# Four early layer-1 halves, experts in pairs, and longer store runs in an attention and expert kernel

## The chip, the core and the metric

The kernel runs on one core of a Trainium2 chip. The metric is the device time of one execution in microseconds; lower is better. The engines of the core are named as in the profile: PE (TensorE, the matmuls; PEld is its weight load), DVE (VectorE), ACT (ScalarE), POOL (GpSimd) and SP (SyncE). Transfers are issued from SP, ACT and POOL and carried out by 16 DMA engines.

## What is computed

Attention over 4 batches, 8 heads, 768 positions and head dimension 64, followed by an expert layer in which each token goes to the one expert that its domain names. Heads 0, 2 and 6 see all earlier positions; the other five see only the first 4 positions (the sinks) and the last 64.

```python
scores = q @ k.T / sqrt(64)             # per batch and head
mask   = causal & (retrieval_head | (pos_k < 4) | (pos_q - pos_k < 64))
x      = softmax(where(mask, scores, -1e9)) @ v      # -> 3072 tokens x 512
for e in range(8):                      # w1[e]: 512 x 1024, w2[e]: 1024 x 512
    rows = domain_id == e
    out[rows] = relu(x[rows] @ w1[e]) @ w2[e]
```

All inputs and the output are fp32 in DRAM.

## The kernel before

Attention is worked off in 16 passes: pass n is a batch (n // 4) with a pair of heads (n % 4). The pairs are (0, 2), (6, 7), (1, 3) and (4, 5). A pass has 6, 5, 3 and 3 rounds, one for each tile of scores of up to 1024 columns (`scores`, L293): mask matmuls, then matmuls of kT and qT into PSUM, then the exponential on ACT into a tile `eT` from `epool`. Between the rounds of pass n TensorE also works off `t_items(n + 1)` (transposes of the next pair's q and k, which DVE copies out as qT and kT) and `av_items(n - 1)` (the exponentials times v, into an accumulator of `ps_a`, which DVE divides by the row sums into `xb`, L398 and L399). `hooks(n)` stands ahead of each pass: it issues the q, k and v loads of pass n + 4 on SP, the casts to fp16 on POOL (L155, L176), and, in some passes, a store of a finished batch (`store_x`, L411, on SP) or a weight load (`load_w`, L181 for the first layer, L187 for the second, on POOL). A weight is 2 MB of fp32 in DRAM and becomes 1 MB of fp16 on its way. The text writes (3,1) for the first-layer weight of expert 3.

The tokens are sorted meanwhile. `routing_items` yields a list of small steps on DVE, among them 24 comparisons of 128 by 128 (`low`, L575), one group of matmuls (`table`) and, at the end, `rows` and `rows2`, which make `map_i` (the row of x for each slot) and `out_i` (the row of the output for each slot). One step is taken after each round from pass 1 on.

The experts work on slots. Each has 448, 384 main and 64 more; a pair of experts has 7 groups of 128 slots: groups 0 to 2 are the main slots of the first expert, 3 to 5 those of the second, 6 the two remainders. `load_xe` (L631) gathers a group's rows of x by an indirect DMA from POOL; `x_transpose` (L647) turns them into `xT`; `layer1` (L671, L678) makes `hT` with relu on ACT; `layer2` (L702) and `layer2_half` (L716) multiply with the second weight, and `finish_group` copies a group of 128 rows out of PSUM into one of four `oute` tiles (L684, on DVE) and scatters it to the output by an indirect DMA from POOL (L686).

The first 256 slots of an expert come from the first three batches, if it has so many tokens there. `N_EARLY` experts use that: their groups 0, 1, 3 and 4 are gathered in pass 14 (with rows of three batches only), and `layer1(e, 0, EARLY)` covers columns 0 to 255 while the last batch's rows are stored and gathered; `layer1(e, EARLY, CAP)` follows. A flag (`flag_i`) tells of an input for which this, or the 448 slots, isn't enough; a loop at the end then does everything again in a plain way.

Nothing is scheduled by a planner: each engine runs its instructions in the order in which the program issues them. POOL's order therefore sets the order of weights, gathers and scatters:

```python
ws = {4: (0, 1), 8: (1, 1), 11: (0, 2), 12: (2, 1)}        # load_w in hooks(n)
if n == 14:
    for g in (0, 1, 3, 4):
        load_xe(0, g, 3)
    load_w(1, 2)
```

After the passes, layer 1 of expert e + 2 is issued ahead of layer 2 of expert e, for each e in turn, and each weight is loaded as soon as its buffer (four for each layer) is free.

Of the kernel before, what the change touches and what calls it, by code (L numbers as in the profile page):

```python
# [9 lines left out]
FP16 = mybir.dt.float16  # L10
# [11 lines left out]
def kernel(  # L22
# [26 lines left out]
    MAIN = 384  # L49
    HALF = CAP - MAIN  # L50
    EARLY = 256
    N_EARLY = 2
    PAIRSLOTS = 2 * CAP
    NSLOT = E * CAP
    PAIRS = [(0, 2), (6, 7), (1, 3), (4, 5)]
# [56 lines left out]
    vpool = ctx.enter_context(tc.tile_pool(name="v32", bufs=4))  # L112
    vepool = ctx.enter_context(tc.tile_pool(name="ve", bufs=2))
    tpool = ctx.enter_context(tc.tile_pool(name="qkT", bufs=2))
    epool = ctx.enter_context(tc.tile_pool(name="eT", bufs=3))
    xpool = ctx.enter_context(tc.tile_pool(name="xb", bufs=2))
    mpool = ctx.enter_context(tc.tile_pool(name="moe", bufs=3))
    opool = ctx.enter_context(tc.tile_pool(name="moe_out", bufs=4))
# [178 lines left out]
    def scores(n, r):  # L297
        chunks, c0, c1 = plans[n % 4][r]
        sp = ps_s.tile([P, 1024], FP32, tag="sp", name=f"sp_{n}_{r}")
        lists = {0: [], 1: [], 2: []}  # L300
        for ch in chunks:
            lists[ch[1]].append(ch)
        order = []
        for a, c in zip(lists[0] + [None] * 8, lists[1] + [None] * 8):
            order += [x for x in (a, c) if x]
        masks = masks_of(n, r)
        begun = set()

        def put(c, w, lhsT, rhs):
            bank = c // 512  # L310
            nc.tensor.matmul(  # L311
                out=sp[:, c : c + w],
                lhsT=lhsT,
                rhs=rhs,
                start=bank not in begun,
                stop=True,
                skip_group_check=True,
            )
            begun.add(bank)

        for c, w, col in masks:
            put(c, w, id_sb, c16[:, col : col + w])
        for c, hh, jt, i0, w in order + lists[2]:
            if hh == 2:
                put(c, w, ks_t[n % 2][:], qT[n][:, i0 : i0 + w])
            else:
                rows = slice(64 * hh, 64 * hh + 64)
                j0 = 0 if jt == "s" else jt * P
                put(c, w, kT[n][rows, j0 : j0 + P], qT[n][rows, i0 : i0 + w])
        if r == 0:  # L330
            eT[n] = epool.tile([P, 6, 1024], FP16, tag="eT", name=f"eT_{n}")
        nc.scalar.activation(  # L332
            out=eT[n][:, r, c0:c1], in_=sp[:, c0:c1], func=AF.Exp, scale=scale
        )

    def masks_of(n, r):
# [15 lines left out]
    def av_items(n):  # L352
# [3 lines left out]
        for hh, h in enumerate(PAIRS[pi]):  # L356
# [15 lines left out]
            def mm(x, h=h, hh=hh, mms=mms, cell=cell, both_s=both_s):  # L372
                it, jt, m0, m1 = mms[x]
                if x == 0:
                    cell["ps"] = ps_a.tile([P, 512], FP32, tag="av", name=f"av_{n}_{hh}")
                ps = cell["ps"][:, 0 : NSO * (D + 1)].rearrange("p (t d) -> p t d", t=NSO)
                r, c = col_of(tiles, hh, jt, it * P + m0)
                w = m1 - m0
                if jt == "s":
                    if both_s and hh == 1:  # L380
                        kk, rhs = slice(32, 36), vs_t[b][32:36, h, :]
                    else:
                        kk, rhs = slice(0, NS), ve_t[b][0:NS, 0, h, :]
                else:
                    kk, rhs = slice(0, P), ve_t[b][:, jt, h, :]
                nc.tensor.matmul(  # L386
                    out=ps[m0:m1, it, :],
                    lhsT=eT[n][kk, r, c : c + w],
                    rhs=rhs,
                    start=(x == 0),  # L390
                    stop=(x == len(mms) - 1),
                    skip_group_check=True,
                )
                if x == len(mms) - 1:
                    if b not in xb:
                        xb[b] = xpool.tile([P, NSO, DM], FP16, tag="xb", name=f"xb_{b}")
                    rcp = tpool.tile([P, NSO], FP32, tag="rcp", name=f"rcp_{n}_{hh}")
                    nc.vector.reciprocal(out=rcp[:], in_=ps[:, :, D])  # L398
                    nc.vector.tensor_tensor(  # L399
                        out=xb[b][:, :, h * D : (h + 1) * D],  # L400
                        in0=ps[:, :, 0:D],
                        in1=rcp[:].unsqueeze(2).to_broadcast([P, NSO, D]),
                        op=ALU.mult,
                    )
# [4 lines left out]

    def store_x(b):  # L410
        nc.sync.dma_start(  # L411
            out=x_d[1 + b * S : 1 + (b + 1) * S, :].rearrange("(t p) d -> p t d", p=P), in_=xb[b][:]
        )


    def routing_items():
# [32 lines left out]
        ohh = mpool.tile([P, NT, 2, NHI], FP16, tag="xT", bufs=4, name="ohh")  # L449
        mf = tile_([P, 2, NHI], FP32, "mf")  # L450
        me = tile_([P, NHI], FP32, "me")

        def one_hot():
            V.tensor_tensor(
# [143 lines left out]

        def rows2():
            V.tensor_scalar(  # L600
                out=mf[:, 1, :], in0=me[:], scalar1=float(NT - 1), scalar2=float(1 - NT),
                op0=ALU.mult, op1=ALU.add,
            )
            V.tensor_tensor(out=mf[:, 1, :], in0=mf[:, 0, :], in1=mf[:, 1, :], op=ALU.add)
            V.tensor_copy(out=map_i[:], in_=mf[:, 1, :])
            V.scalar_tensor_tensor(
                out=me[:], in0=me[:], scalar=2.0 * NTOK, in1=mf[:, 1, :],
                op0=ALU.mult, op1=ALU.add,
            )
            V.tensor_scalar(  # L610
                out=out_i[:], in0=me[:], scalar1=1.0, scalar2=None, op0=ALU.subtract
            )

        idle = lambda: None
# [2 lines left out]
            add(fn)  # L617
        for t in range(0, NT, 2):
            add(lambda t=t: (low(t), low(t + 1)))
        for fn in (idle, table, rows, rows2):  # L620
            add(fn)
        return items

    xe_t, xT_t, hT_t = {}, {}, {}
    NG = PAIRSLOTS // P

    def load_xe(pr, g, nb=B):
        if pr not in xe_t:
            xe_t[pr] = vepool.tile([P, NG, DM], FP16, tag="ve", name=f"xe_{pr}")
        s = pr * NG + g  # L630
        nc.gpsimd.indirect_dma_start(  # L631
            out=xe_t[pr][:, g, :],
            out_offset=None,
            in_=x_d[0 : 1 + nb * S, :],
            in_offset=bass.IndirectOffsetOnAxis(ap=map_i[:, s : s + 1], axis=0),
            bounds_check=nb * S,
            oob_is_err=False,
        )

    def x_transpose(pr, g):  # L640
# [4 lines left out]
        for c in range(4):  # L645
            c1, r = divmod(c, 2)
            nc.tensor.transpose(  # L647
                out=ps[:, c, :],
                in_=xe_t[pr][:, g, c1 * 256 + r : (c1 + 1) * 256 : 2],
                identity=id_sb,  # L650
            )
        if g < 6:
# [8 lines left out]

    def layer1(e, c0, c1):
        if e not in hT_t:
            hT_t[e] = epool.tile([P, 8, CAP], FP16, tag="eT", name=f"hT_{e}")
        for f2 in range(4):
            ps = ps_s.tile([P, 1024], FP32, tag="sp", name=f"h1_{e}_{f2}_{c0}")
            pv = ps[:].rearrange("p (a c) -> p a c", a=2)
# [83 lines left out]
    def hooks(n):  # L751
# [9 lines left out]
            vs_copy(b)  # L761
        if n >= 5 and n % 4 == 1:
            store_x(n // 4 - 1)
        ws = {4: (0, 1), 8: (1, 1), 11: (0, 2), 12: (2, 1)}
        if n in ws:
            load_w(*ws[n])
        if n == 14:
            for g in (0, 1, 3, 4):
                load_xe(0, g, 3)
            load_w(1, 2)  # L770

    for _, fn in t_items(0):
        fn()
    route = routing_items()
    for n in range(NPAIR + 1):
        if n < NPAIR:
            hooks(n)
# [8 lines left out]
        for r in range(R):  # L786
            if n < NPAIR:
                scores(n, r)
            if n >= 1 and route:
                route.pop(0)()  # L790
            while x < len(bg) and (done < total * (r + 1) / R - 1 or r == R - 1):
                done += bg[x][0]
                bg[x][1]()
                x += 1
        if n == NPAIR - 1:
            for g in (0, 1, 3, 4):
                x_transpose(0, g)

    store_x(B - 1)
    for g in (2, 6, 5):  # L800
        load_xe(0, g)
    for e in range(N_EARLY):
        layer1(e, 0, EARLY)
    load_w(3, 1)
    for g in range(4):
        load_xe(1, g)
    load_w(2, 2)
    for g in range(4, NG):
        load_xe(1, g)
    for g in (2, 6, 5):  # L810
        x_transpose(0, g)
    for e in range(N_EARLY):
        layer1(e, EARLY, CAP)
        load_w(e + 4, 1)
        if e == 0:
            load_w(3, 2)
    for e in range(E):
        pr, i = divmod(e, 2)
        nxt = e + 2
        if i == 1:  # L820
            layer2_half(pr)
        if nxt < E:
            if i == 0:
                for g in range(7):
                    x_transpose(pr + 1, g)
                if pr + 2 < E // 2:
                    [load_xe(pr + 2, g) for g in range(NG)]
            layer1(nxt, 0, CAP)
            if nxt + 4 < E:
                load_w(nxt + 4, 1)  # L830
        layer2(e)
        if e + 4 < E:
            load_w(e + 4, 2)


    with tc.If(nc.values_load(flag_i[0:1, 0:1], min_val=0, max_val=2) > 0, preferred_fallthrough_block=False):  # L836
        with tc.For_i(0, NT, 1) as t:
            g_d64 = rpool.tile([P, 1], I64, name="g_d64")
            nc.sync.dma_start(
                out=g_d64[:], in_=moe_domain_id[bass.ds(t * P, P)].rearrange("(p c) -> p c", c=1)  # L840
# [1 line left out]
            g_dom = rpool.tile([P, 1], FP32, name="g_dom")  # L842
            nc.vector.tensor_copy(out=g_dom[:], in_=g_d64[:].bitcast(I32)[:, 0:1])
            gx = vepool.tile([P, DM], FP16, tag="ve", name="gx")
            nc.sync.dma_start(out=gx[:], in_=x_d[bass.ds(t * P + 1, P), :])
            gps = ps_t.tile([P, NSO, P], FP16, tag="tp", name="gps")
            for c in range(4):
                c1, r = divmod(c, 2)
# [81 lines left out]
```

## Time and profile before

| What | Value |
|---|---|
| median of 5 runs | 241.78 us (240.82 to 242.83) |
| profiled execution | 242.02 us, of which 240.2 us are the span from the first to the last instruction |
| mean granted TensorE clock | 0.935 |
| PE, PEld busy | 203.2 us (85%), 120.5 us (50%) |
| DVE, ACT, POOL busy | 105.6, 92.7, 110.3 us |
| POOL's DMA queue | 26.75 MB, 48.5% of the 16 engines' span |
| SP's DMA queue | 22.02 MB, 33.5% |
| L671 PE, first layer | 320 matmuls, 53.1 us |
| L702 PE, second layer | 192 matmuls, 42.6 us |
| L631 POOL, gathers | 28, 28.4 us of issue |
| L686 POOL, scatters | 28, 27.9 us of issue |

A row of the page names line, engine and operation, what is written and read, then busy time, the mean of one and the idle time of the engine ahead of it with its releaser. In the rows for a stretch of time the columns are its length, then for each engine (PE, PEld, DVE, ACT, POOL) the busy time and the number of instructions, then the granted clock of TensorE as a share, the share of the DMA engines that was busy, and GB/s. Attention ends at 109 us on TensorE, and its last matmul of all ends at 231.5 us.

### The profile page before, as it was taken

Reading aid. Unit: us, or ns where it says so; the run is one execution under the profiler, and the core shown is the slowest. Engines: PE = TensorE matmul, PEld = TensorE weight load, DVE = VectorE, ACT = ScalarE, POOL = GpSimd, SP = SyncE. Lnnn points to the kernel's source line nnn. Section 1 sums busy time; section 2 is a strip of 40 time slices with the busy share of each in tenths; the row PEclk is TensorE's granted clock in tenths of the full one; section 3 lists DMA queues with packets and bytes.
Section 4 is the critical chain, followed back from the end, with each engine's and each line's share of the span. In section 5 each row is a group of like instructions: output and inputs, shape, how many; then the busy total and the mean of one; then the engine's idle time right before and its main releaser. Section 6 shows DMA issues by size and latency. Waiting matters only on the chain. (4 is left out here: it accounts for less than half of the span.)

```text
span 240.2 us, 4605 instructions
## 1 busy us (share of the span) xinstructions
PE 203.2 (85%) x1871; PEld 120.5 (50%) x1871; DVE 105.6 (44%) x242; ACT 92.7 (39%) x109; POOL 110.3 (46%) x143
## 2 busy tenths in 40 slices
PE   1489969996999999989582699997999889999950
PEld 0246545664556666669471354545545455454420
DVE  1349999997546956761202203125040431303330
ACT  2177538762647687635260041320505023140000
POOL 0647565454413760701778612737545321505540
PEclk9999998998559999999998579999999999999996
DMA  6999999999999998285499999999977873303320
GB/s 220 297 317 290 286 287 248 298 334 285 232 301 299 268 191 220 66 165 168 96 252 221 198 213 263 149 263 220 277 226 182 212 158 68 134 3 122 130 107 23
DMA packets 45467, 49.77 MB, mean 207 GB/s; under 512 B 27263, under 2 KB 38784, under 8 KB 45442
## 3 DMA queue, kind: packets, MB, share of 16 engines
q0 software_dynamic: 7936, 26.75, 48.5%
q1 hardware_dynamic: 36928, 22.02, 33.5%
q10 hardware_dynamic: 578, 0.66, 0.9%
q8 instruction: 16, 0.26, 0.4%
q14 instruction: 9, 0.07, 0.1%
HBM read 56.76 MB, written 10.49 MB: 280 GB/s over the span
## 5 line engine op out<-in xcount | busy, mean ns | idle before, releaser
L332 ACT ACTIVATE eT<-sp 128x1024 f16<-128x1024 f32 (+2 forms) x68 | 60.7, 916 | 39.1 <-PE sp L311 38.5
L678 ACT ACTIVATE hT<-h 128x896 f16<-128x896 f32 (+2 forms) x40 | 30.7, 768 | 79.6 <-PE h L671 79.6
L671 PE MATMUL h<-xT,w 128*128 128x448 f16 (+2 forms) x320 | 53.1, 326 | 1.2 <-DVE xT L657 1.2
L686 POOL DMA_INDIRECT out_dram<-oute,out_i x28 | 27.9, 995 | 39.3 <-DVE oute L684 36.4
L684 DVE COPY oute<-o 128x512 f32<-128x512 f32 x24 | 16.6, 692 | 66.5 <-PE o L702 66.5
L631 POOL DMA_INDIRECT xe<-x_tok,map_i x28 | 28.4, 1015 | 33.5 <-SPq L836 10.8
L671 PEld LDWEIGHTS <-w 128*128 128x128 f16 x320 | 34.1, 115 | 19.1 <-issue 4.1
L702 PE MATMUL o<-w,hT 128*128 128x512 f16 x192 | 42.6, 379 | 0.0
L386 PE MATMUL av<-ve,eT 128*128 128x65 f16 (+3 forms) x532 | 32.3, 199 | 2.8 <-DVE xb L399 2.8
L386 PEld LDWEIGHTS <-eT 128*128 128x128 f16 (+3 forms) x572 | 26.2, 102 | 14.0 <-issue 4.6
L311 PE MATMUL sp<-qT,kT 64*128 64x192 f16 (+6 forms) x244 | 27.7, 291 | 3.1 <-DVE fl L542 1.9
L702 PEld LDWEIGHTS <-hT 128*128 128x128 f16 x192 | 18.7, 98 | 22.4 <-issue 0.4
L155 POOL CAST q<-q 128x768 f16<-128x768 f32 x15 | 12.9, 862 | 32.7 <-issue 13.0
L311 PE MATMUL sp<-c16s 128*128 128x128 f16 (+1 forms) x132 | 26.6, 285 | 0.6 <-ACT eT L332 0.5
L647 PE MATMUL xtp<-c16s,xe 128*128 128x128 f16 x112 | 10.5, 228 | 12.4 <-DMA xe<-x_tok,map_i 9.5
L281 DVE COPY qT<-tpq 128x768 f16<-128x768 f16 x16 | 15.3, 955 | 8.3 <-PE tpq L276 8.3
L311 PEld LDWEIGHTS <-kT 64*128 64x128 f16 x244 | 9.9, 96 | 18.0 <-issue 7.5
L155 POOL CAST k<-k 128x768 f16<-128x768 f32 x16 | 13.5, 843 | 11.0 <-DMA k<-in_k_dram 9.4
L399 DVE TENSOR_TENSOR xb<-av,rcp 128x384 f16<-128x384 f32 x32 | 17.8, 557 | 1.1
L654 DVE COPY xT<-xtp 128x512 f16<-128x512 f16 x24 | 9.3, 420 | 19.8 <-PE xtp L647 18.8
L281 DVE COPY kT<-tpk 128x768 f16<-128x768 f16 x16 | 15.2, 949 | 3.5 <-PE tpk L276 3.5
L176 POOL CAST ve<-v 128x384 f16<-128x384 f32 x32 | 15.9, 525 | 0.7 <-DMA v<-in_v_dram 0.7
(71 smaller groups left out, 124.5 us busy)
## 6 DMA issues: line engine op xcount, KB each, us to landing
w<-in_moe_w_dram POOLq DMA_DIRECT2D x16, 1024.0 KB, 10.4
q<-in_q_dram SPq DMA_DIRECT2D x16, 384.0 KB, 6.0
k<-in_k_dram SPq DMA_DIRECT2D x16, 384.0 KB, 6.0
v<-in_v_dram SPq DMA_DIRECT2D x32, 192.0 KB, 5.9
x_tok<-xb SPq DMA_DIRECT2D x4, 768.0 KB, 5.9
xe<-x_tok,map_i POOLq DMA_INDIRECT x28, 7.2
out_dram<-oute,out_i POOLq DMA_INDIRECT x28, 2.8
c16s<-c ACTq DMA_DIRECT2D x1, 336.5 KB, 4.5
```

What stands on the lines that cost most here:

```text
L155: eng.tensor_copy(out=t[:].rearrange("p t h d -> p h t d"), in_=q32_t[nm, n][:])
L281: nc.vector.tensor_copy(out=d[:], in_=cell["ps"][:].rearrange("d t p -> d p t"))
L311: nc.tensor.matmul(out=sp[:, c : c + w], lhsT=lhsT, rhs=rhs, start=bank not in begun, stop=True, skip_group_check=True,)
L332: nc.scalar.activation(out=eT[n][:, r, c0:c1], in_=sp[:, c0:c1], func=AF.Exp, scale=scale)
L386: nc.tensor.matmul(out=ps[m0:m1, it, :], lhsT=eT[n][kk, r, c : c + w], rhs=rhs, start=(x == 0), stop=(x == len(mms) - 1), skip_group_check ...
L399: nc.vector.tensor_tensor(out=xb[b][:, :, h * D : (h + 1) * D], in0=ps[:, :, 0:D], in1=rcp[:].unsqueeze(2).to_broadcast([P, NSO, D]), op=A ...
L631: nc.gpsimd.indirect_dma_start(out=xe_t[pr][:, g, :], out_offset=None, in_=x_d[0 : 1 + nb * S, :], in_offset=bass.IndirectOffsetOnAxis(ap= ...
L671: nc.tensor.matmul(out=pv[:, a, c0:c1], lhsT=w_t[e, 1][:, c // 2, c % 2, fc * 512 + fr : (fc + 1) * 512 : 4], rhs=xT_t[e][:, c, c0:c1], st ...
L678: nc.scalar.activation(out=hT_t[e][:, 2 * f2 : 2 * f2 + 2, c0:c1], in_=pv[:, :, c0:c1], func=AF.Relu)
L684: nc.vector.tensor_copy(out=o[:], in_=ps[:])
L686: inst = nc.gpsimd.indirect_dma_start(out=out, out_offset=bass.IndirectOffsetOnAxis(ap=out_i[:, s : s + 1], axis=0), in_=o[:], in_offset=None,
L702: nc.tensor.matmul(out=ps[:], lhsT=hT_t[e][:, f, g * P : (g + 1) * P], rhs=w_t[e, 2][:, f // 4, f % 4, :], start=(f == 0), stop=(f == 7),)
```

## The change

It has these parts.

- `N_EARLY` becomes 4: experts 0 to 3 do their first 256 columns ahead. The early gathers of pairs 0 and 1 stand in pass 14, each pair's four followed by a weight, (2,1) and (3,1). Weights (0,2), (2,1) and (1,2) leave passes 11, 12 and 14.
- The gathered rows get other buffers (`xe_of`: those of q and k for groups 0 to 5, those of v for group 6). The early ones are cleared by four memsets on DVE in pass 14.
- The transposes of pair 0's early groups move from ahead of the last attention matmuls to behind them.
- Experts go in pairs: both layer 2 of a pair, then the loads, then both layer 1 of the pair after the next. In POOL's queue (4,1), (2,2), (5,1) and (3,2) stand one behind the other, and so do (6,1), (4,2), (7,1) and (5,2).
- x is stored so that each partition's six rows lie together: 6 KB in one run, where it was 1 KB. `rows2` and the new `rows3` compute the row of x for it.
- The routing takes a step in two of three rounds.
- `epool` has five smaller buffers instead of three; `eT` of a pass takes one or two of them.
- POOL gets a drain behind the last two weights.

```diff
-    N_EARLY = 2
+    N_EARLY = 4
-    epool = ctx.enter_context(tc.tile_pool(name="eT", bufs=3))
+    epool = ctx.enter_context(tc.tile_pool(name="eT", bufs=5))
...
-        if r == 0:
-            eT[n] = epool.tile([P, 6, 1024], FP16, tag="eT", name=f"eT_{n}")
+        if r % 3 == 0:
+            t = epool.tile([P, 8 * CAP], FP16, tag="eT", name=f"eT_{n}_{r}")
+            eT[n, r // 3] = t[:, 0 : 3 * 1024].rearrange("p (r c) -> p r c", r=3)
...
     def store_x(b):
         nc.sync.dma_start(
-            out=x_d[1 + b * S : 1 + (b + 1) * S, :].rearrange("(t p) d -> p t d", p=P), in_=xb[b][:]
+            out=x_d[1 + b * S : 1 + (b + 1) * S, :].rearrange("(p t) d -> p t d", p=P), in_=xb[b][:]
         )
...
+    def xe_of(pr, g):
+        u, o = (2 * pr + g // 3, g % 3) if g < 6 else ((pr, "h"), 0)
+        if u not in xe_t:
+            if g < 6:
+                xe_t[u] = qkpool.tile([P, 3, DM], FP16, tag="qk"[u % 2], name=f"xe_{u}")
+            else:
+                xe_t[u] = vpool.tile([P, 1, DM], FP16, tag="v32", name=f"xeh_{pr}")
+        return xe_t[u][:, o, :]
...
-        ws = {4: (0, 1), 8: (1, 1), 11: (0, 2), 12: (2, 1)}
+        ws = {4: (0, 1), 8: (1, 1)}
         if n in ws:
             load_w(*ws[n])
         if n == 14:
-            for g in (0, 1, 3, 4):
-                load_xe(0, g, 3)
-            load_w(1, 2)
+            for pr in range(2):
+                for i in range(2):
+                    xe_of(pr, 3 * i)
+                    nc.vector.memset(xe_t[2 * pr + i][:, 0:2, :], 0.0)
+            for pr in range(2):
+                for g in (0, 1, 3, 4):
+                    load_xe(pr, g, 3)
+                load_w(2 + pr, 1)
...
             if n >= 1 and route:
-                route.pop(0)()
+                rounds += 1
+                if rounds % 3:
+                    route.pop(0)()
...
-        if n == NPAIR - 1:
-            for g in (0, 1, 3, 4):
-                x_transpose(0, g)
-
     store_x(B - 1)
-    for g in (2, 6, 5):
-        load_xe(0, g)
-    for e in range(N_EARLY):
-        layer1(e, 0, EARLY)
-    load_w(3, 1)
...
+    for g in (0, 1, 3, 4):
+        x_transpose(0, g)
+    for g in (2, 5, 6):
+        load_xe(0, g)
+    load_w(0, 2)
+    for g in (2, 5, 6):
+        load_xe(1, g)
+    load_w(1, 2)
+    for g in range(NG):
+        load_xe(2, g)
+    layer1(0, 0, EARLY)
+    for g in (0, 1, 3, 4):
+        x_transpose(1, g)
+    for e in range(1, N_EARLY):
+        layer1(e, 0, EARLY)
...
+    for pr in range(2):
+        for g in (2, 5, 6):
+            x_transpose(pr, g)
+        for e in (2 * pr, 2 * pr + 1):
+            layer1(e, EARLY, CAP)
+            if e < 2:
+                load_w(e + 4, 1)
+                load_w(e + 2, 2)
+    for pr in range(E // 2):
+        a, b_ = 2 * pr, 2 * pr + 1
+        layer2(a)
+        layer2_half(pr)
+        layer2(b_)
+        for e in (a, b_):
+            if e + 6 < E:
+                load_w(e + 6, 1)
+            if e + 4 < E:
+                load_w(e + 4, 2)
+        if pr == 1:
+            nc.gpsimd.drain()
+        if pr + 3 < E // 2:
+            for g in range(NG):
+                load_xe(pr + 3, g)
+        if pr + 2 < E // 2:
+            for g in range(NG):
+                x_transpose(pr + 2, g)
+            layer1(a + 4, 0, CAP)
+            layer1(b_ + 4, 0, CAP)
```

`rows2` and `rows3` have ten small DVE operations together, where `rows2` had five; the loop at the end reads x by the new order.

## The prediction

> **What bounds the kernel now.** I read the page first (busy tenths, clock, DMA), then the stretches by engine and clock, the waits of TensorE, its timeline from 100 us on, and last the issues and landings of the GpSimd queue. The page:
>
> ```profile
> span 240.2 us, 4605 instructions
> PE   1489969996999999989582699997999889999950
> DVE  1349999997546956761202203125040431303330
> PEclk9999998998559999999998579999999999999996
> DMA  6999999999999998285499999999977873303320
> ```
>
> TensorE (203.2 us busy of 240.2) is the bound nearly everywhere, so the question is where it idles and where its clock is low. Two holes show: slices 5, 6 and 9 with the half clock of slices 11 and 12, and slices 19 to 23. The DMA row is near full up to slice 31 and offers no free room before 180 us. The stretches:
>
> ```profile
> 20.00:40.00 20.00, 16.95 (x229) 10.69 (x228) 19.22 (x51) 11.36 (x13) 13.11 (x21) 0.91 1.12 284
> 40.00:60.00 20.00, 17.80 (x267) 11.59 (x265) 18.14 (x54) 11.73 (x14) 8.60 (x14) 0.97 1.11 299
> ...
> 58.80:72.40 13.60, 13.60 (x109) 7.71 (x107) 6.51 (x15) 7.23 (x8) 4.07 (x6) 0.50 1.10 270
> 130.50:140.70 10.20, 7.10 (x27) 3.32 (x28) 1.34 (x4) 0.92 (x1) 6.02 (x6) 0.50 1.05 208
> ```
>
> From 20 to 60 us VectorE (fourth column, 37.4 of 40 us) is full while TensorE idles 5.2 us: the routing shares VectorE with attention. Then TensorE is busy for 13.6 us at half clock. The second half-clock stretch follows the hole in the expert stage:
>
> ```profile
> PE xtp L647 <- DMA xe<-x_tok,map_i: 9.5, 6, 4.5
> ...
> 131.74 1.03 PE L647 MATMUL xtp<-c16s,xe 128*128 128x128 f16 x8 [4.52 <-DMA xe<-x_tok,map_i]
> 134.25 0.61 PE L647 MATMUL xtp<-c16s,xe 128*128 128x128 f16 x4 [1.48 <-DMA xe<-x_tok,map_i]
> 135.24 8.90 PE L671 MATMUL h<-xT,w 128*128 128x448 f16 x32 [0.39 <-DVE xT L657]
> ...
> 151.11 6.24 PE L671 MATMUL h<-xT,w 128*128 128x448 f16 x32
> ```
>
> Between 115 and 136 us TensorE waits 9.5 us for gathered rows, and the first full layer 1 takes 8.90 us instead of 6.24: 2.7 us more for the clock. All gathers, weights and scatters go through one GpSimd queue:
>
> ```profile
> 127.85 0.79 POOL L181 DMA_DIRECT2D w<-in_moe_w_dram  x1
> 128.59 0.81 POOL L187 DMA_DIRECT2D w<-in_moe_w_dram  x1
> 129.32 0.79 POOL L181 DMA_DIRECT2D w<-in_moe_w_dram  x1
> ...
> 126.00:130.00 4.00, 1.07 (x12) 0.71 (x12) 1.57 (x4) 0.00 (x0) 3.69 (x5) 1.00 1.06 214
> ```
>
> With weights alone in flight the core moves 214 GB/s, and a weight is 1.05 MB as stored: 4.9 us each. The third of these weights lands 19.6 us after its issue (148.9), a gather issued behind it at 131.79 lands 17.9 us after its own: the queue delivers in order. A lone weight takes 8.1 us to landing, a lone gather 2.8, a lone scatter 2.7. A scatter issued at 155.24 behind one weight took 11.0.
>
> **The change, part by part.**
>
> 1. Routing in two rounds of three (rounds % 3). Routing costs VectorE some 19 us up to the table matmul: 24 ohl at 0.32 us (7.7) and single operations of 0.13 to 0.93. Before, all of that and the first row step lie in passes 1 to 7; now about 15.3 us do, the rest moves to passes 8 to 11: 4.4 us less for VectorE before 58 us. Passes 10 and 11 are short: 4.1 to 4.5 us of TensorE each against about 4 of VectorE without routing (qT and kT 0.95 each, ks 0.3, two of 0.20 plus 0.56, vs 0.3), and get rows, rows2 and rows3 (13 operations of some 0.18). That gives back about 1.4. Net -3.0. Bounds: 0, if the transfers pace attention (q15 lands at 81.6 and its cast runs at 86.0 now, so only 4.4 us of slack), and -5.5, if the half-clock stretch of 58.8 to 72.4 goes with the idle time before it. At 109 matmuls in 13.6 us against about 14.5 per us at full clock that stretch costs some 6 us, which the slack caps.
>
> 2. Four memsets of xe (hook 14) on VectorE. From the rows of 64 and 256 words (112 and 272 ns), 512 words take about 0.49: 1.95 us in the queue ahead of qT and kT of pass 15. 0.62 us of idle time stands there; kT then ends at about 100.3, its first use is at 100.78. The softmax division at 99.59 ends 1.3 late and holds an accumulator: +0.4. Without that cover, +1.9. The first gather waits for the first memset and starts near 97.2, against 96.74.
>
> 3. Transposes of pair 0 behind the last attention matmuls: 1.82 us of TensorE (104.38 to 106.20) move out of the path to the last store, so attention ends at 106.2 and the store goes out at 107.1; in SP's queue nothing stands behind it. No work is saved.
>
> 4. The 6 KB runs. Now the store of 0.79 MB lands 3.7 us after issue on an idle DMA, 6.0 among other transfers; the stretch that moves it runs at 348 GB/s with 1 KB runs. The Trainium skill (DMA: Bandwidth & Descriptors, Specifications) holds that 512 bytes are already enough for line rate. By the row the longer run can save at most a few tenths of the 2.3 us of transfer, by the rule nothing. I take nothing. Against it: the store now meets weights (2,1) and (3,1) in flight, which it did not before. I take 5 us (between 3.7 and 6.0).
>
> 5. Early halves for four experts. Each costs 3.62 us (7.24 for two now); the halves are 0.2 us dearer than a whole layer 1 per expert, 0.4 for the two new ones. In the time of this trace: attention 106.2, transposes 108.1, half 0 111.7; pair 1's early gathers lie behind weight (2,1), issued at 102.4 and landing at 110.5, the last gather at 112.0: wait 0.4; transposes 114.0; halves 1 to 3 124.9; the last batch's gathers, behind (3,1), have landed by 119; transposes 126.9; two rests of 2.84 132.6; transposes 134.6; rests 140.3. The 9.5 us of waiting are gone.
>
> 6. Weights and scatters. GpSimd issues the gathers of pairs 0, 1 and 2 (1.3 us each) with (0,2) and (1,2) until 132, then (4,1), (2,2), (5,1), (3,2) in a row. They land at about 140, 145, 150 and 155. Layer 2 of expert 0 runs from 140.3 to 145.5 and its scatters are issued at once, but stand behind these four weights: they land from 155. There are four oute buffers; the fifth copy (expert 1, first group) waits for the first scatter. With two accumulators TensorE then stops at the third group of expert 1, at 150.9, for 5.1 us. Now the same fifth copy waits for one weight only and its wait ends as its matmuls do (159.0). Afterwards (6,1), (4,2), (7,1), (5,2) are issued behind the last scatter of pair 0, from 160; they land until 182.5, pair 3's gathers until 185, scatters of pair 1 behind them (the first is also held at its issue until (5,2) has landed, since each issue of this queue waits for the eighth before it): 1.8 us of waiting at 184.6. Pair 3's transposes (188.1) find their rows. The end of TensorE is 229.1 with a store of 6 us, 228.2 with 5, against 231.5.
>
> 7. The clock after that stop. The skill (TensorE: Matmul & The Clock Gate, Part 1) lets the clock fall to half after one idle window of about 3.4 us and return after one busy one: 1.7 us lost. The trace shows less mercy: after the idle 4.5 us the clock stayed at 0.50 for 10.2 us, about 5 lost if all of it is work. A stop of 5.1 us should trip it. A slower TensorE also eats the 1.8 us of waiting that comes later. I take +1.5, between 0 and +5.
>
> 8. The drain after (7,2): GpSimd's next work is a scatter some 20 us later. Nothing; were it on the path, one issue, 1 us. The fallback loop isn't entered: in the drawn input the first four experts have 285 to 311 tokens in three batches, and none has over 448. epool has five buffers, eT takes six per four passes and always finds one free.
>
> **Sum.** Against the profiled run (240.2 us span, 242.02 us with what lies around it): 231.5 to 228.2 is -3.3, attention -3.0, memsets +0.4, clock +1.5: -4.4, so 235.8 span and 237.6. The median of the runs is 241.78, 0.24 under that run: 237.4.
>
> **Rivals.** (a) The half clock in attention goes too and the stop at 151 us stays short (the store lands in 3.7): attention -5.5, expert stage -4.6, memsets +0.4, clock +0.7: -9.0, so 232.8. For it: the idle 2.4 us of 53 to 58 stand directly before the fall. Against: the DMA row is full there.
> (b) Slower: the scatters behind four weights. If a weight takes 5.6 us beside scatters and gathers instead of 4.9 (154 to 157 us ran at 162 GB/s), the eight that stand before expert 0's scatters come 5.6 us later, the stop is 10.7 us, and the clock costs its 5: with attention -1, 241.8 - 3.3 + 5.6 + 5 + 0.4 - 1 = 248; with half of that, 245. It decides from about 9 us of stop and slow clock together.
> (c) No change: the routing only moves its pressure to passes 8 to 11 (0 instead of -3), the rest as computed, with the clock at +3: 241.8.
>
> **How the numbers follow.** The likeliest, 0.40, gives 237.4 (its own range 235 to 239.5); (a) 0.26; (b) 0.21; (c) 0.13. A measurement here tells apart about 0.5%, 1.2 us. Faster: 0.40 + 0.26 and a little of (c): 0.68; same 0.11; slower 0.21. The range from 231.5 to 245 takes in most of (a) and the lower half of (b).
>
> **What would show it.** Right: attention's last matmuls by 104; no wait on gathers between 110 and 136; VectorE's copies of oute for expert 1 waiting for a scatter near 150, with TensorE idle 3 to 5 us and the clock low behind it; (6,1) issued after 157. Wrong: no such wait of oute (the queue is not in order, or the weights landed sooner), or no shorter attention, or transposes of pair 1 still waiting for rows.

## The result and the profile after

The changed kernel takes 241.51 us (median of 42 runs, 237.99 to 248.34), the kernel before 241.60 (79 runs); the ratio is 0.995 [0.993, 0.997]. Ratios leave disturbed runs out, so they need not be the ratio of the medians, and oute7_shifted below, with too few undisturbed runs, has none. Forecast: 237.4, -1.8%. Measured: -0.5%. Two later comparisons of the same two kernels gave 0.991 [0.987, 0.995] and 0.990 [0.984, 0.996].

The page of the changed kernel (its own time 241.94 us, its span 240.1):

```profile
PE   1489989699989999999988994068999479999990
DVE  1347999999969768532022040025003160033431
PEclk9999999999997999959999998559999999999997
DMA  6999999999999431799799899935999649813322
```

The holes at slices 19 to 22 (counted from 0) are gone. In their place stands one at slices 24 to 26, deeper than any before, with the half clock behind it, and a small one near slice 31. The DMA row now has a gap of its own at slices 13 to 15, and is full from there to slice 24. By stretches (length; busy time and instructions of TensorE, weight loads, VectorE, ScalarE, GpSimd; granted clock; DMA share; GB/s):

```profile
20.00:40.00 20.00, 18.67 (x268) 12.09 (x265) 17.82 (x51) 13.62 (x17) 12.24 (x21) 1.00 1.13 288
40.00:60.00 20.00, 17.96 (x257) 11.27 (x254) 19.52 (x47) 13.01 (x15) 11.60 (x18) 1.00 1.12 304
80.00:98.00 18.00, 17.44 (x249) 10.93 (x247) 13.13 (x28) 13.16 (x16) 8.38 (x11) 1.00 0.21 72
98.00:157.00 59.00, 46.65 (x427) 36.98 (x427) 11.30 (x28) 19.17 (x34) 26.52 (x28) 0.87 0.98 210
100.90:107.80 6.90, 6.66 (x50) 5.06 (x48) 2.87 (x8) 0.66 (x2) 2.78 (x3) 0.51 1.04 280
148.70:162.40 13.70, 4.20 (x16) 2.00 (x16) 1.92 (x3) 0.00 (x0) 1.97 (x2) 0.50 0.71 181
```

From 20 to 60 us TensorE idles 3.4 us where it was 5.2. From 80 to 98 us the DMA carries 72 GB/s; from 98 to 157 it is full at 210 GB/s. That is the queue that the stop hangs on. TensorE's timeline:

```profile
110.84 10.74 PE L701 MATMUL h<-xT,w 128*128 128x256 f16 x96
...
135.84 5.34 PE L732 MATMUL o<-w,hT 128*128 128x512 f16 x24
...
142.96 3.63 PE L732 MATMUL o<-w,hT 128*128 128x512 f16 x16
158.20 3.57 PE L732 MATMUL o<-w,hT 128*128 128x512 f16 x8 [11.61 <-DVE oute L714]
...
191.63 1.89 PE L732 MATMUL o<-w,hT 128*128 128x512 f16 x8 [3.24 <-DVE oute L714]
...
228.77 5.36 PE L732 MATMUL o<-w,hT 128*128 128x512 f16 x24
```

The early halves run without a wait for rows. Layer 2 of expert 1 stops for 11.6 us on a copy of oute, and expert 3 for 3.2. The waits say what that copy waited for. The landings of the three scatters of expert 0 from 138 to 144 us say how long those took, the one below them that of the last of the four weights ahead of them in the queue, and the last that of attention's last store:

```profile
DVE oute L714 <- DMA out_dram<-oute,out_i: 19.5, 3, 13.7
PE o L732 <- DVE oute L714: 14.8, 2, 11.6
```

```profile
L716 POOL DMA_INDIRECT out_dram<-oute,out_i x3: 982/1039/1068, 138.7 to 142.2; - x3
...
DMA to landing us min/median/max: 16.4/17.5/18.6
...
L187 POOL DMA_DIRECT2D w<-in_moe_w_dram x1: 750/750/750, 134.2 to 134.2; - x1
...
DMA to landing us min/median/max: 22.4/22.4/22.4
...
L412 SPq DMA_DIRECT2D x_tok<-xb x1: 357/357/357, 102.9 to 102.9; - x1
...
DMA to landing us min/median/max: 7.8/7.8/7.8
```

The span in three parts, before and after: to attention's last matmul 108.11 and 102.07 us (-6.04); from there to the last matmul of all 123.35 and 132.05 (+8.70); from there to the end 8.78 and 5.94 (-2.84). Together -0.2. A second profile of the changed kernel (after_again, 239.23 us) has 99.7, 131.9 and 5.7 us, with a stop of 10.9 us. The third part is the surprise: it lies behind all work, and is GpSimd's last drain (durations min/median/max in ns). Before, and then after, with the added drain first:

```profile
L925 POOLq DRAIN  x3: 46/109/6100, 233.3 to 240.0; - x3
```

```profile
L868 POOLq DRAIN  x1: 16961/16961/16961, 195.3 to 195.3; - x1
...
L970 POOLq DRAIN  x3: 50/103/2932, 236.3 to 239.8; - x3
```

### The profile page after: what moved, and what is told of

Read it like the earlier page. It is cut to its first block, busy times and chain, and to the rows that moved or that the text cites. A ratio compares the mean times of both kernels' runs of the same rounds, so it can differ in the third digit from the quotient of the medians.

```text
span 240.1 us, 4769 instructions
## 1 busy us (share of the span) xinstructions
PE 200.3 (83%) x1935; PEld 125.3 (52%) x1935; DVE 107.5 (45%) x251; ACT 93.6 (39%) x117; POOL 110.1 (46%) x143
## 5 line engine op out<-in xcount | busy, mean ns | idle before, releaser
L708 ACT ACTIVATE hT<-h 128x512 f16<-128x512 f32 (+2 forms) x48 | 32.1, 668 | 78.4 <-PE h L701 78.4
L732 PE MATMUL o<-w,hT 128*128 128x512 f16 x192 | 44.6, 390 | 14.8 <-DVE oute L714 14.8
L701 PE MATMUL h<-xT,w 128*128 128x256 f16 (+2 forms) x384 | 52.2, 297 | 1.6 <-DVE xT L686 1.6
L701 PEld LDWEIGHTS <-w 128*128 128x128 f16 x384 | 39.7, 115 | 13.2 <-DVE xT L686 1.7
L660 POOL DMA_INDIRECT xe<-x_tok,map_i x24 | 24.4, 1018 | 26.0 <-DVE xe L801 7.8
L387 PE MATMUL av<-ve,eT 128*128 128x65 f16 (+3 forms) x532 | 31.4, 197 | 5.0 <-DVE xb L400 3.1
L311 PE MATMUL sp<-qT,kT 64*128 64x192 f16 (+6 forms) x244 | 26.1, 277 | 1.4 <-DVE kT L281 1.4
L311 PE MATMUL sp<-c16s 128*128 128x128 f16 (+1 forms) x132 | 25.9, 277 | 0.4 <-ACT eT L333 0.2
L276 PE MATMUL tpq<-c16s,q 128*128 128x128 f16 x96 | 9.4, 237 | 6.0 <-DVE q L155 5.2
## 6 DMA issues: line engine op xcount, KB each, us to landing
w<-in_moe_w_dram POOLq DMA_DIRECT2D x16, 1024.0 KB, 11.6
```

What stands on the lines that cost most here:

```text
L311: nc.tensor.matmul(out=sp[:, c : c + w], lhsT=lhsT, rhs=rhs, start=bank not in begun, stop=True, skip_group_check=True,)
L387: nc.tensor.matmul(out=ps[m0:m1, it, :], lhsT=eT[n, r // 3][kk, r % 3, c : c + w], rhs=rhs, start=(x == 0), stop=(x == len(mms) - 1), skip ...
L660: nc.gpsimd.indirect_dma_start(out=xe_of(pr, g), out_offset=None, in_=x_d[0 : 1 + nb * S, :], in_offset=bass.IndirectOffsetOnAxis(ap=map_i ...
L701: nc.tensor.matmul(out=pv[:, a, c0:c1], lhsT=w_t[e, 1][:, c // 2, c % 2, fc * 512 + fr : (fc + 1) * 512 : 4], rhs=xT_t[e][:, c, c0:c1], st ...
L708: nc.scalar.activation(out=hT_t[e][:, 2 * f2 : 2 * f2 + 2, c0:c1], in_=pv[:, :, c0:c1], func=AF.Relu)
L732: nc.tensor.matmul(out=ps[:], lhsT=hT_t[e][:, f, g * P : (g + 1) * P], rhs=w_t[e, 2][:, f // 4, f % 4, :], start=(f == 0), stop=(f == 7),)
```

## The experiments

They ran on five chips, A to E, each with the kernel before beside them. "Halves to layer 2" is the time in the profile from the start of the halves of experts 1 to 3 to the start of layer 2; in the changed kernel it is 25.0 (110.84 to 135.84).

| kernel | chip | median us | ratio to before | halves to layer 2 |
|---|---|---|---|---|
| oute7 | A | 237.0 | 0.984 [0.976, 0.992] | 29.4 |
| two_behind | A | 243.3 | 1.004 [0.999, 1.009] | 30.0 |
| weights_early | A | 254.9 | 1.056 [1.044, 1.069] | 32.2 |
| route_each | A | 254.8 | 1.052 [1.043, 1.062] | 30.2 |
| before_route23 | B | 240.8 | 0.999 [0.995, 1.003] | |
| before_oute6 | B | 242.9 | 0.993 [0.989, 0.997] | |
| w02_early | B | 250.0 | 1.032 [1.026, 1.039] | 34.7 |
| oute7_w02 | B | 240.1 | 0.990 [0.987, 0.994] | 34.5 |
| w2_shifted | C | 242.7 | 1.004 [0.998, 1.010] | 29.1 |
| oute7_shifted | C | 239.6 | none | 30.6 |
| store_1k | C | 250.5 | 1.024 [1.015, 1.034] | 31.9 |
| no_drain | C | 251.8 | 1.039 [1.030, 1.048] | 29.5 |
| before_drain | D | 238.6 | 0.987 [0.981, 0.992] | |
| oute7_no_drain | D | 232.3 | 0.960 [0.954, 0.965] | 25.0 |
| after_again | D | 239.9 | 0.991 [0.987, 0.995] | 25.0 |
| oute7_again | D | 229.7 | 0.948 [0.943, 0.954] | 25.0 |
| after_third | E | 239.9 | 0.990 [0.984, 0.996] | 25.0 |
| store_1k_again | E | 243.4 | 1.000 [0.995, 1.004] | 25.0 |

The last column falls into two groups: 25.0 on D and E, 29 to 35 on A to C. Only kernels of one chip are compared below, until the last section takes this up.

### Is the stop what swallowed the gain?

Seven oute buffers let TensorE pass while scatters are under way:

```diff
-    opool = ctx.enter_context(tc.tile_pool(name="moe_out", bufs=4))
+    opool = ctx.enter_context(tc.tile_pool(name="moe_out", bufs=7))
```

> The changed kernel with seven oute tiles instead of four, nothing else. Theory A (TensorE stops for 11.6 us in layer 2 of expert 1 because the fifth copy into oute waits for the first scatter, which stands behind four weights in GpSimd's queue): the stop goes, and the one of 3.2 us at 188 us too; (6,1) is issued when (3,2) has landed, near 157 instead of 163.8, pair 3's rows arrive near 183 and become the next wait, 3 to 5 us. Total 230 to 233 us. Theory B (the DMA queue alone sets the pace and the oute tiles only show it): the wait moves to (6,1), (7,1) or pair 3's rows, and the total stays over 238.

> Seven oute buffers on the changed kernel once more, for an interval: 236 to 238.5, ratio 0.975 to 0.99; if the first result was a lucky one: 240 or more.

On A it came out between the two theories; on D, beside the changed kernel as it is (0.991), it is at 0.948, below the range expected: the stops cost 10.2 us there. TensorE's timeline of the second run:

```profile
143.20 5.35 PE L732 MATMUL o<-w,hT 128*128 128x512 f16 x24
...
181.62 3.19 PE L676 MATMUL xtp<-c16s,xe 128*128 128x128 f16 x24 [4.71 <-DMA xe<-x_tok,map_i]
```

Experts 0 and 1 run through; what is left is a wait of 4.7 us for pair 3's rows behind the late weights. The control, six buffers in the kernel before (seven do not fit), is the same edit in that kernel, whose trace has no wait of TensorE on a copy of oute.

> The kernel before with six oute buffers instead of four (seven do not fit into its SBUF). Theory A (the stop at layer 2 of experts 0 and 1 is brought in by the change): the trace of before shows no wait of TensorE on a copy of oute, so nothing moves: 240.5 to 243. Rival I (more oute buffers are worth something in either kernel, and the gain of seven in the changed kernel says nothing on the change): below 239.

```diff
-    opool = ctx.enter_context(tc.tile_pool(name="moe_out", bufs=4))
+    opool = ctx.enter_context(tc.tile_pool(name="moe_out", bufs=6))
```

It gave 0.993: more than the nothing of theory A, but a sixth of what the buffers are worth in the changed kernel. The stop is the change's own.

Moving two of the four weights behind layer 2 of expert 0 takes the scatters past them:

```diff
-            if e < 2:
-                load_w(e + 4, 1)
-                load_w(e + 2, 2)
+            if e == 0:
+                load_w(4, 1)
+                load_w(2, 2)
...
         layer2(a)
+        if pr == 0:
+            load_w(5, 1)
+            load_w(3, 2)
         layer2_half(pr)
```

> The changed kernel with the weights (5,1) and (3,2) issued behind the three scatters of expert 0 instead of ahead of them. Theory A (order in the queue): expert 0's scatters stand behind two weights and land near 146 to 148, the stop of 11.6 us in layer 2 of expert 1 shrinks to 0 to 2 us, no half clock follows, total 230 to 234 us. Theory B (DMA throughput sets the pace): the weights land no sooner, the wait returns at layer 1 of expert 5 or at pair 3's rows, total over 238.

The stop at expert 1 went, and one of 9.1 us came at expert 3, since the late weights now stood before the scatters of pair 1. It is 2% slower than seven buffers on the same chip. The bytes only changed their place in the queue.

### Could the transfers have run earlier?

The DMA is nearly idle from 80 to 98 us. The first trial moved (0,2) and (2,1) there, and (3,1) behind all eight early gathers:

```diff
-        ws = {4: (0, 1), 8: (1, 1)}
+        ws = {4: (0, 1), 8: (1, 1), 11: (0, 2), 12: (2, 1)}
...
-                load_w(2 + pr, 1)
+            load_w(3, 1)
...
-    load_w(0, 2)
```

> The changed kernel with (0,2) and (2,1) loaded in passes 11 and 12 again, as in the kernel before; all else as changed. Theory C (the change leaves the DMA engines idle from 80 to 98 us and pushes two weights of 4.9 us each into the stretch in which they are full): everything in the queue from the last store on comes some 10 us earlier, the store of the last batch meets one weight less, expert 0's scatters land near 146, the stop shrinks from 11.6 us to 0 to 3, total 228 to 232 us. Theory D (the order of four weights in a row is the cause, whatever stood before them): the stop stays at 8 us or more, total over 237.

The second moved (0,2) alone, and the third was the same with seven oute buffers:

```diff
-        ws = {4: (0, 1), 8: (1, 1)}
+        ws = {4: (0, 1), 8: (1, 1), 11: (0, 2)}
...
-    load_w(0, 2)
```

> The changed kernel with weight (0,2) issued in pass 11, where the kernel before had it, instead of behind the rests of pair 0. Theory C (the queue from 98 to 157 us is full with transfers that could have run between 80 and 98 us, where the DMA is idle): 5 us of transfer leave the full stretch, the scatters of expert 0 land near 152.5 instead of 157.3, the stop of 11.6 us falls to 6 or 7: 235 to 238.5. Theory D (what made the run with three early weights slow also follows from one, such as a later end of attention): 243 or more.

> Both seven oute buffers and weight (0,2) in pass 11, on the changed kernel. Theory A (once no copy of oute waits for a scatter, the end of the weights' queue near 157 us holds nothing more): within 0.4% of seven buffers alone, 236 to 238. Theory C (the full queue still delays layer 1 and the late weights): 232 to 235.5. Theory D: 240 or more.

The first two were slower than before, 1.056 and 1.032, and theory C fell. The stop at expert 1 was shorter, 5.9 us in w02_early and 5.5 in weights_early, but not because the scatters landed sooner: in w02_early it ended at 164.6 us, later than the 158.2 of the changed kernel, and theory C had the scatters down near 152.5. It was shorter because TensorE came to it later. Layer 2 began at 148 us instead of 136, for TensorE had stopped in the halves:

```profile
120.89 1.03 PE L701 MATMUL h<-xT,w 128*128 128x256 f16 x8 [1.08 <-issue]
123.79 5.32 PE L701 MATMUL h<-xT,w 128*128 128x256 f16 x32 [1.87 <-ACT hT L708]
...
147.96 5.34 PE L732 MATMUL o<-w,hT 128*128 128x512 f16 x24
```

The waits are put down to nothing that the profile shows, or to engines that themselves were waiting for TensorE. GpSimd issues gathers from 114.5 to 132 us meanwhile. The four weights then waited for TensorE to free a buffer: (4,1) was issued at 138.4 us, and from 133 to 139 us the DMA was 9% busy. From that issue to the end of the stop it took 26 us, as in the changed kernel (132.1 to 158.2). With seven buffers the same edit gave 0.990, so the buffers were worth 4.1% here too; the time, 240.1, is theory D's. The fourth trial left a weight in front of each run of gathers:

```diff
-    load_w(0, 2)
+    load_w(1, 2)
     for g in (2, 5, 6):
         load_xe(1, g)
-    load_w(1, 2)
+    load_w(2, 2)
...
-                load_w(e + 2, 2)
+                if e == 1:
+                    load_w(3, 2)
```

> The changed kernel with weight (0,2) in pass 11, and (1,2) and (2,2) each one place earlier, so that both runs of gathers behind the last store still stand behind a weight as in the changed kernel (with (0,2) alone moved, they met an idle DMA, and TensorE had stops of 1 to 2 us between 118 and 134 us, with 15.8 us for the halves 1 to 3 instead of 10.7). Theory J (those stops come with gathers that run while no weight is in flight): the halves take 10.7 us again, three weights instead of four stand before the scatters of expert 0, the stop of 11.6 us is 5 to 7: 234 to 238 us. Theory K (a weight issued in pass 11 is itself what harms): halves of 14 us or more, 244 or more.

> The same with seven oute buffers. Theory J: no stop at layer 2 of expert 1, the late weights 4 us earlier than with seven buffers alone: 232 to 236. Theory K: 240 or more, as with seven buffers and (0,2) alone (240.1).

The halves took 11.1 us (114.58 to 125.69), near theory J's 10.7, but from 130 us on TensorE stopped again, 29.1 us in all. The DMA was full then (share 1.01 from 130 to 136 us, with a weight issued at 125.5), so theory J, gathers that run while no weight is in flight, does not explain the stops. The stop at expert 1 took 3.9 us and ended at 158.3, where that of the changed kernel ends: again TensorE only came later. The times, 242.7 and 239.6, lie between the theories. Whether early weights are worth something without such stops was not tried on D or E.

### What is the routing worth?

In the kernel before, alone:

```diff
+    rounds = 0
...
-                route.pop(0)()
+                rounds += 1
+                if rounds % 3:
+                    route.pop(0)()
```

> The kernel before with one part of the change alone: the routing takes its step in two rounds of three. Theory G (the part is worth what it shortens attention by, where nothing else holds the end): attention's last matmul moves from 108.4 to about 104, the last store and the gathers behind it follow, and all later issues of the GpSimd queue hang on that store: 236.5 to 238.5 us. Theory H (the routing only moves its pressure to passes 8 to 11, or the waits for gathered rows between 115 and 136 us swallow the gain): 240.5 to 242.5.

Nothing: 0.999 [0.995, 1.003]. The half clock of 58.8 to 72.4 us is gone (clock 1.00, 208 matmuls in that stretch instead of 109), and the third store leaves at 87.2 us instead of 91.5, but attention ends at 107.0 instead of 108.1. GpSimd's timeline:

```profile
90.40 0.82 POOL L155 CAST q<-q 128x768 f16<-128x768 f32 x1 [10.56 <-DMA q<-in_q_dram]
```

Attention reaches its weight issues 5 us earlier (73.9 and 79.1 us), and the cast of the last q waits 10.6 us for its transfer (before: it waited for TensorE alone, at 86.0). A wait for transfers took the place of the one for VectorE. In the changed kernel those two weights are issued at 115.2 and 97.2 us, and the gain comes through. That the weights make the wait is argued from this: with both back in their passes (weights_early) the last cast of q waited 5.7 us for its transfer, with (0,2) alone (oute7_w02) 5.9, and in the changed kernel no cast of q more than 2.5. The opposite test, one step in every round of the changed kernel:

```diff
-                rounds += 1
-                if rounds % 3:
-                    route.pop(0)()
+                route.pop(0)()
```

> The changed kernel with a routing step after every round again. Attention then ends some 4 us later (106 instead of 101.9). Theory E (attention's gain is lost at the stop in layer 2 of expert 1, whose end is set by the queue): the stop is shorter by about as much, and the total stays within 1 us of the changed kernel (241 to 243). Theory F (attention is on the path): total 245 to 246.

Slower than both theories: 1.052. Attention ended at 110.0 us and the stops were 8.2 and 3.2. Theory E fails in its mechanism too: the first stop ended at 166.7 us, 56.7 after attention's end, where the changed kernel has 56.1. The end of the stop moves with attention. The changed kernel was not on that chip; if seven buffers are worth there what they are on D (0.991 to 0.948), it stood near 1.028, and the routing in every round then costs some 2.4%. That is an estimate.

### The drain

Left out of the changed kernel, and of the one with seven buffers:

```diff
-        if pr == 1:
-            nc.gpsimd.drain()
```

> The changed kernel without the drain behind weight (7,2). Step 8 (it costs nothing: GpSimd's next work comes 20 us later): 240.5 to 243, the trace of 190 to 220 us unchanged. Rival (it holds GpSimd until the scatters before it have landed[...]): more than 1 us to either side.

> Seven oute buffers on the changed kernel, and no drain. Theory L: 2.9 us more than seven buffers with the drain, all of it behind the last matmul: 239 to 241.5. If the 6.7 us that the last matmul came later without the drain belong to the missing drain itself and not to the stop at layer 2: 245 or more.

And put alone into the kernel before:

```diff
         if e + 4 < E:
             load_w(e + 4, 2)
+        if e == 3:
+            nc.gpsimd.drain()
```

> The kernel before with one part of the change alone: GpSimd drained once behind the issue of weight (7,2). Theory L (the drain at the end of the kernel takes time for every GpSimd transfer since the last drain; an earlier one beside other work takes most of it off the end): the final drain falls from 6.1 us to about 3, the rest is as before: 237.5 to 239.5 where before is 241.6 (ratio about 0.988). Step 8 of the forecast (nothing): within 0.5% of before. Rival (the drain delays scatters of expert 4 and, through four oute buffers, TensorE): slower by 1% or more.

0.987 [0.981, 0.992], with the last drain at half its length:

```profile
L927 POOLq DRAIN  x3: 46/109/3035, 234.4 to 238.0; - x3
```

With seven buffers on D, leaving it out costs 0.960 against 0.948, 2.7 us, and the last drain is 6.02 us instead of 3.24. So the gain that theory L forecast is there: some 3 us of GpSimd's last drain move off the end. That no_drain stood at 1.039 on C is not the drain: its last matmul came 6.7 us late, the halves and rests took 29.5 us, and oute7_no_drain on D shows 25.0.

### The store, and the changed kernel itself

The old store, the old row arithmetic and no rows3:

```diff
-            out=x_d[1 + b * S : 1 + (b + 1) * S, :].rearrange("(p t) d -> p t d", p=P), in_=xb[b][:]
+            out=x_d[1 + b * S : 1 + (b + 1) * S, :].rearrange("(t p) d -> p t d", p=P), in_=xb[b][:]
...
-        for fn in (idle, table, rows, rows2, rows3):
+        for fn in (idle, table, rows, rows2):
```

> The changed kernel with the store in 1 KB runs and the row arithmetic of the kernel before. If the run length is worth nothing (step 4): within 0.5% of the changed kernel, 240.5 to 243, with a last store that lands some 8 us after its issue as there. If the 6 KB runs save descriptors and so transfer time among weights: the store lands 1 us or more later, 243 to 245. If the five row operations in passes 10 and 11 are what costs: 239 or less.

> The changed kernel with the store in 1 KB runs and the row arithmetic of before. Theory M and step 4 (the run length is worth nothing): within 0.6% of the changed kernel in the same job, on either kind of chip. If the 1 KB store itself cost the 2.4%: 1.02 of before while the changed kernel is at 0.99.

> The changed kernel, unchanged, beside the 1 KB store. Theory M (the stops of TensorE beside runs of gather issues come with the chip, not with the edit): either 0.99 of before with no stop of TensorE put down to issue between 90 and 140 us, as in the last job, or 1.02 to 1.03 with them. If the edits made the stops: 0.99 whatever the chip.

> The changed kernel, unchanged, as a control in the same job. If its distance from the kernel without the drain (251.8) is real: ratio to before 0.99 to 1.0 again, 240.5 to 243. If chip and day made that distance: 246 or more.

On E it is at 1.000 beside 0.990: the 6 KB runs, with their five operations, seem to gain about 1%, but the intervals just overlap. The last store landed 9.7 us after its issue instead of 8.6 in after_third; with 6 KB runs that time itself lies between 6.8 and 8.6 us in the five profiles of the first comparison, D and E. What the store takes arrives in expert 1's stop, since the gathers and weights behind it wait for it:

| run | store to landing, us | attention's end, us | stop at expert 1, us |
|---|---|---|---|
| after_again | 6.8 | 99.7 | 10.9 |
| after | 7.8 | 102.1 | 11.6 |
| after_third | 8.6 | 102.6 | 12.6 |
| store_1k_again | 9.7 | 99.8 | 13.7 |

The stop follows the store and not attention's end. On C alone one would have read 2.4% into the run length.

## Why the prediction was wrong, point by point

**Step 1, the routing (-3.0): within its bounds here, but not by itself.** With the memsets the prediction has attention's end at 103.6 us; it came at 102.1. The half clock of 58.8 to 72.4 us went too (clock 1.00, 195 matmuls instead of 109), which rival (a) had and the likeliest case did not. (Counted from 0, as the holes are, the low tenths of that clock stand at slices 10 and 11, not 11 and 12.) The bound of 0 was the right one for this part alone, for the reason given (transfers with 4.4 us of slack). What the working missed is that two parts of the change need each other: the weights had to leave passes 11 and 12.

**Steps 2, 3 and 5: right.** The memsets took 0.49 us each, and a wait of TensorE of 0.45 us for a division follows them. The transposes moved as worked out, the 9.5 us of waits for rows are gone, and halves 1 to 3 take 10.74 us, near the 10.9 of the working. Half 0 fell into a half clock that the trace of before did not show there: 5.46 us instead of 3.62.

**Step 4, the store (nothing gained, landing 5 us): the landing wrong, the gain open.** It landed 7.8 us after issue, with two weights in flight beside it; 5 lay too near the idle row of 3.7, and the other bound, 6.0, was too low as well. The working followed the Trainium skill (DMA: Bandwidth & Descriptors, Specifications), where 512 bytes are enough for line rate. The 1 KB store landed 1.1 us later than the 6 KB one on the same chip, in one profile of each; that is less than the 1.8 us by which the 6 KB store differs between profiles, so the runs do not show the rule to be wrong.

**Step 6, the scatters: the step that failed.** The mechanism was right: the fifth copy of oute waits for the first scatter, behind four weights. What was mis-sized is the time of the queue. Both sides of the stop start from attention's last matmul. From there TensorE reached the third group of expert 1 after 44.5 us (102.1 to 146.6); the working, whose timeline leaves the gain of the routing to the sum, has 44.7 (106.2 to 150.9). The first scatter was down after 55.2 us (157.3); the working has 48.8 (155). The stop, which is the difference with 1 us for what follows the landing, was 11.6 us instead of 5.1. Of the 6.5 us more, 2.8 are the last store (7.8 us instead of 5), on which the first gather waits. Some 1.5 lie between its landing and the issue of (4,1), 21.4 us instead of 19.9: (4,1) went out at 132.1, when (1,2), eight issues before it, had landed (131.5). The other 2.2 lie between that issue and the first scatter, 25.2 instead of 23: the last two weights took 5.6 us each, rival (b)'s price.

The clock times of the landings, (4,1) at 140.8, (2,2) at 145.5 and (3,2) at 156.6, look close to the forecast, but by luck: attention had ended 4.1 us earlier than in that timeline, and the queue had lost about as much again. The gain of attention as such was not lost in the stop, for the queue hangs on the last store and so on attention's end. "The DMA row offers no free room before 180 us" held for the kernel before and not for this one: the change itself emptied 80 to 98 us, and those transfers came back in front of the scatters.

**Step 7, the clock (+1.5): about right.** Work resumed at 158.2 and the full clock was back at 162.4. The eight matmuls in it took 3.57 us where eight of the sixteen before the stop took 1.8, and the eight transposes behind them 1.01 instead of 0.61: 2.2 lost. The estimate of 1.7 that the prediction worked out from the Trainium skill (TensorE: Matmul & The Clock Gate, Part 1) is near it; the one busy window of about 3.4 us was 4.2 in this trace. The 5 of the other bound did not come: in the kernel before, waits of 1.5 and 0.4 us followed the first, and here work went on without them.

**Step 8, the drain (nothing): wrong, and in the other direction.** I asked what the drain delays, and not what a drain does to the next one. It is worth some 3 us.

**The sum.** Predicted span 235.8. Attention ended 1.5 earlier than that; attention's end to last matmul took 132.1 us instead of 123.5 (+6.5 first stop, +1.4 second, +1.8 half 0, the rest small and of both signs); the end -2.8. 235.8 - 1.5 + 8.6 - 2.8 = 240.1, the measured span. Rival (b) had the mechanism and nearly the size (10.7 us of stop), though only part of it came from the weights' price. It was priced slower than before for lack of the drain's gain and with less of attention's, and its terms add up to 248.5, not 248.

## What to carry to other kernels

A wait is the difference of two times, and both often start at the same event: give both from that event on, here attention's end, and the wait is what is left. A gain ahead of the event moves both; what must be priced well is the longer of the two. A queue that delivers in order should be read as one list, each entry with its size, and every result that must leave through it (here scatters, and through them the output buffers) stands at the end of that list. Before pricing a change in one run, give the part alone and the whole kernel the same chip: the same kernel stood at 0.984 of before on one and 0.948 on another.

## What was not expected

GpSimd's drain at the end of the kernel took 6.02 to 6.10 us where no other came before it (before, before_oute6, no_drain, oute7_no_drain), and 2.73 to 3.24 where one had come behind (7,2) (after, after_again, after_third, before_drain, oute7_again). The early one took 17.0 us in the changed kernel, all beside TensorE's work. What it empties the runs do not show; that its time goes with the transfers since the last drain is argued, not shown.

TensorE's stops beside runs of gather issues were in all ten profiles of changed-kernel variants on A, B and C, and in none of the six on the others (the first profile, D and E). With them, halves to layer 2 took 29 to 35 us; in the other six, 25.00 to 25.02. Attention's tail from the first gather took 11.6 to 15.0 us in nine of the ten and 8.8 in oute7_shifted, and 9.6 to 10.1 in the six. The two kernels that ran on both kinds, seven buffers and the 1 KB store, were 3.7% and 2.5% slower beside the stops, by their ratios to before. The kernel before felt them less: its medians are 242.9 to 244.2 us on A to C and 241.7 and 241.6 on D and E. Its two variants on B show small ones as well, such as a wait of 0.6 us for ACT inside the rests of experts 0 and 1, which run unbroken in before and before_drain.

So the stops go with the chip, or with its state at that time, and not with the edit. One thing more tells the two kinds apart, whatever the kernel: in none of the twelve profiles from A to C is the landing of any GpSimd transfer recorded, and in the eight others they are. All this is inferred from one stay on each chip, and the changed kernel as it is was not set beside the variants on A, B or C. What makes TensorE stop stays open: the profile puts the waits down to nothing it shows, or to engines that were themselves waiting for TensorE.

The best version here is the changed kernel with seven oute buffers: 0.948 [0.943, 0.954] on D, 0.984 [0.976, 0.992] on A.
